# An attention block beside an MLP on one core: the MLP's second product by Strassen's algorithm, value products that leave PSUM batch by batch, mish in one bank, weights laid out by tiles

## The chip, the cores and the metric

The kernel runs on one core of one Trainium2 chip. The metric is the device time of one execution in microseconds; lower is better. Its engines are TensorE (PE; PEld is its weight load), VectorE (DVE), ScalarE (ACT), GpSimd (POOL) and SyncE (SP), which here only issues transfers (DMAs). Each engine works through its own instructions in order, and waits on semaphores for the others.

## The reference

```
xn = layernorm(x)                                  # x: 2048 x 1024
q, k, v = split(xn @ wqkv)                         # 32 heads of 32
s = concat(softmax(q k^T / sqrt(32)) v) @ wo
h = xn @ w1 + b1                                   # w1: 1024 x 3584
g = silu((h * tanh(softplus(h))) @ w2)             # mish; w2: 3584 x 1024
out = x + s * g
```

All of it is float32. The kernel splits each operand of a large product into a high and a low part in a shorter format (float32r) and adds three products (high x high, high x low, low x high): the constant THREE in the code. So a product of two 128 x 128 by 128 x 512 tiles is three matmuls.

## The kernel before

**Stages.** First the layer norm, the transposition of xn and the value projection (v, L324); meanwhile GpSimd splits the first 20 of 28 column tiles of w1 and stores the parts in DRAM (w1_early, w1s). Then the projections of q and k (qk, L623), 16 tiles f of four groups c of 24 matmuls; meanwhile GpSimd splits the other eight w1 tiles and all of w2 (presplit), and the parts go to DRAM (w2s). Then the main stage, in which attention and the MLP run interleaved. At last the output projection (op, L1113) with the gate, 768 matmuls.

**The main stage** is ordered by a planner written in the kernel (class Plan). Each engine has a list of operations with an assumed duration, what they need, which places of which ring they take and give (buffers and PSUM banks), and a due time; the planner plays this through and emits the instructions in the order that results. That order is then fixed for each engine. TensorE draws from five streams: s (scores by query, for the maxima, L694), t (scores by key, L781), h (first MLP product, L929), y (second MLP product, L1017), and at the end op.

**Attention.** For each head and each of 16 key tiles, t is made in four banks, ScalarE takes the exponential into a tile p of 128 x 2048 (L264), GpSimd adds p to the head's sum z (L810, 15 additions a head), and TensorE multiplies p with v (pv, L828) in three batches of 6, 5 and 5 key tiles (GROUPS), all into bank 7, which is kept for this. A p tile is free when both its addition and its batch are done. When the last addition of a head is done, TensorE multiplies z with ones (zp, L854) for the softmax denominator; there is one z tile, so the next head's first addition (z<-p,p) waits for that product. VectorE finds the maxima of s (mx, L700).

**MLP.** For each of four chunks of 512 rows and each of 28 column tiles of w1, h is made in 24 matmuls in one bank; mish is a chain of five ScalarE and seven VectorE operations (L948 to L984) which takes a second bank, q; its result is the pair of parts act. Two act tiles together are multiplied with two row tiles of w2: eight banks of six matmuls each, added to yacc by VectorE (L1037). w1 is read back in tiles of 1 MB with two places, w2 in tiles of 512 KB with five.

**Places.** w1_tile gives the split tiles of w1 and the qk weights (qkw) one of two places each. In the qk stage a group's result is copied by ScalarE (qst), its low part is taken by VectorE, and a DMA of ScalarE's queue stores it; the next tile's weights are split by ScalarE and VectorE in qk_split, which is written behind the first group of the tile before.

## Time and profile before

| | us |
|---|---|
| median of the runs (lowest, highest) | 3427.83 (3426.24, 3431.74) |
| the profiled execution | 3429.67 |
| its span, from the first to the last instruction | 3427.8 |
| TensorE busy | 3395.9 |
| GpSimd busy | 2461.5 |
| VectorE busy | 2320.4 |
| ScalarE busy | 1943.1 |
| first qk matmul (end of the v stage) | 214.64 |
| first output matmul of the last stage | 3248.98 |

All numbers of the prediction come from this one profiled execution. Its rows have these forms. A group of instructions: line, engine, operation, written tile <- read tiles, shape, count | busy us, mean ns of one | idle us of the engine just before them, and what ended most of it. A row of the timeline: start, length, engine, line, operation, tiles, count, and in brackets the idle time before it with the releaser. A row of a window: length; busy us and (count) of TensorE, its weight loads, VectorE, ScalarE, GpSimd; granted clock of TensorE; busy share of the 16 DMA engines; GB/s.

### The profile page before, as it was taken

Reading aid. Unit: us, or ns where it says so; the run is one execution under the profiler, and the core shown is the slowest. Engines: PE = TensorE matmul, PEld = TensorE weight load, DVE = VectorE, ACT = ScalarE, POOL = GpSimd, SP = SyncE. Lnnn points to the kernel's source line nnn. Section 1 sums busy time; section 2 is a strip of 40 time slices with the busy share of each in tenths; the row PEclk is TensorE's granted clock in tenths of the full one; section 3 lists DMA queues with packets and bytes.
Section 4 is the critical chain, followed back from the end, with each engine's and each line's share of the span. In section 5 each row is a group of like instructions: output and inputs, shape, how many; then the busy total and the mean of one; then the engine's idle time right before and its main releaser. Section 6 shows DMA issues by size and latency. Waiting matters only on the chain.

```text
span 3427.8 us, 47242 instructions
## 1 busy us (share of the span) xinstructions
PE 3395.9 (99%) x17827; PEld 2541.0 (74%) x17827; DVE 2320.4 (68%) x3750; ACT 1943.1 (57%) x3112; POOL 2461.5 (72%) x753
## 2 busy tenths in 40 slices
PE   8999999999999999999999999999999999999999
PEld 8998888676777777776777667777777777676787
DVE  6012236877878887887877777878788787874533
ACT  6111112666666667666666676666666666667621
POOL 0644342898888888888888788888888888888800
PEclk9999999999999999999999999999999999999999
DMA  8988897433433354343433543333435443433482
GB/s 290 299 297 299 295 316 236 124 107 91 124 111 111 99 164 147 109 120 103 124 111 111 159 137 111 111 110 113 127 104 167 131 129 109 116 113 129 151 289 85
DMA packets 294183, 529.71 MB, mean 155 GB/s; under 512 B 88810, under 2 KB 147178, under 8 KB 270186
## 3 DMA queue, kind: packets, MB, share of 16 engines
q1 hardware_dynamic: 274100, 484.74, 46.1%
q10 hardware_dynamic: 19856, 41.95, 3.3%
q8 instruction: 141, 2.31, 0.3%
q14 instruction: 86, 0.70, 0.1%
HBM read 386.89 MB, written 138.67 MB: 153 GB/s over the span
## 4 chain that ended last, share of the span: by engine, by line
PE 96%; DVE 1%; DMA 1%; ACT 1%; issue 0%; SPq 0%; POOL 0%; POOLq 0%
PE h L929 17%; PE y L1017 17%; PE t L781 13%; PE s L694 13%; PE pv L828 13%; PE qk L623 10%; PE op L1113 5%; PE v L324 5%; PE zp L854 1%; DVE mx L700 1%; PE s L550 0%; DMA qstack<-qs 0%; PE pt L379 0%; SPq L271 0%; DMA xr<-xs 0%
## 5 line engine op out<-in xcount | busy, mean ns | idle before, releaser
L810 POOL TENSOR_TENSOR z<-z,p 128x2048 f32<-128x2048 f32 x448 | 2065.4, 4610 | 197.4 <-ACT p L264 170.3
L264 ACT ACTIVATE p<-t,zero 128x512 f32<-128x512 f32 x2048 | 1377.6, 688 | 696.5 <-PE t L781 687.5
L700 DVE TENSOR_REDUCE mx<-s 128x1 f32<-128x512 f32 x1984 | 1318.6, 686 | 445.8 <-PE s L694 444.0
L1017 PE MATMUL y<-w,act 128*128 128x512 f32 x2688 | 928.3, 391 | 1.2 <-DVE yacc L1037 0.5
L781 PE MATMUL t<-qstack,kstack 128*128 128x512 f32 x2048 | 791.0, 392 | 3.3 <-DMA qstack<-mt 1.9
L694 PE MATMUL s<-kstack,qstack 128*128 128x512 f32 x1984 | 773.2, 395 | 9.8 <-issue 4.8
L929 PE MATMUL h<-xr,w 128*128 128x512 f32 x2016 | 698.5, 391 | 1.5 <-DMA xr<-xs 1.3
L1017 PEld LDWEIGHTS y<-w,act 128*128 128x128 f32 x2688 | 503.7, 188 | 115.0 <-issue 5.0
L694 PEld LDWEIGHTS s<-kstack,qstack 128*128 128x128 f32 x1984 | 368.0, 188 | 136.4 <-issue 43.3
L828 PE MATMUL pv<-p,v 128*32 128x512 f32 x4096 | 459.4, 595 | 0.0
L781 PEld LDWEIGHTS t<-qstack,kstack 128*128 128x128 f32 x2048 | 384.7, 188 | 97.1 <-issue 9.9
L929 PEld LDWEIGHTS h<-xr,w 128*128 128x128 f32 x2016 | 378.8, 188 | 84.1 <-issue 4.3
L623 PE MATMUL qk<-xc,qkw 128*128 128x512 f32 x1536 | 350.9, 390 | 0.0
L810 POOL TENSOR_TENSOR z<-p,p 128x2048 f32<-128x2048 f32 x32 | 147.9, 4621 | 261.8 <-ACT p L264 154.2
L828 PEld LDWEIGHTS pv<-p,v 128*32 128x32 f32 x4096 | 123.5, 110 | 282.2 <-issue 281.9
L623 PEld LDWEIGHTS qk<-xc,qkw 128*128 128x128 f32 x1536 | 288.3, 188 | 59.7
L1037 DVE TENSOR_TENSOR yacc<-yacc,y 128x512 f32<-128x512 f32 x416 | 283.1, 681 | 50.2 <-PE y L1017 49.0
L929 PE MATMUL h<-xc,w 128*128 128x512 f32 x672 | 233.1, 392 | 0.0
L275 DVE TENSOR_TENSOR qst<-qk,qst 128x512 fp32r<-128x512 f32 x64 | 44.2, 691 | 245.3 <-ACT qst L267 245.3
L267 ACT ACTIVATE qst<-qk 128x512 fp32r<-128x512 f32 x64 | 38.3, 598 | 300.1 <-PE qk L623 253.9
L324 PE MATMUL v<-vw,xc 128*128 128x256 f32 x1536 | 191.1, 286 | 2.5 <-POOL vw L275 1.5
L324 PEld LDWEIGHTS v<-vw,xc 128*128 128x128 f32 x1536 | 186.9, 193 | 4.1 <-POOL vw L275 1.9
(91 smaller groups left out, 2279.1 us busy)
## 6 DMA issues: line engine op xcount, KB each, us to landing
w<-w1s SPq DMA_DIRECT2D x112, 1024.0 KB
w<-w2s SPq DMA_DIRECT2D x224, 512.0 KB
w2s<-pw SPq DMA_DIRECT2D x56, 512.0 KB
qstack<-qs SPq DMA_DIRECT2D x96, 256.0 KB
kstack<-ks SPq DMA_DIRECT2D x96, 256.0 KB
w1s<-w1p SPq DMA_DIRECT2D x20, 1024.0 KB
praw<-in_B_w_dram SPq DMA_DIRECT2D x72, 256.0 KB
x<-in_A_x_dram SPq DMA_DIRECT2D x32, 512.0 KB
```

Source lines behind the costliest of these rows:

```text
L264: nc.scalar.activation(out_, in_, fn, bias=zero if bias is None else bias, scale=scale)
L324: nc.tensor.matmul(ps[:, :256], xc[t // 4][:, a, k, (t % 4) * P:(t % 4 + 1) * P], w[:, b, k], start=n == 0, stop=n == 3 * KT - 1)
L623: nc.tensor.matmul(ps, w[:, a, k], xc[c][:, b, k], start=n == 0, stop=n == 3 * KT - 1)
L694: nc.tensor.matmul(sp_, qst[h % 3][:, qt * P:(qt + 1) * P], kst[h % 3][:, kc * 512:(kc + 1) * 512], start=True, stop=True)
L700: nc.vector.reduce_max(tiles["mx"][:, qt, kc:kc + 1], tiles[qt, kc], axis=AX.X)
L781: nc.tensor.matmul(tp, kst[h % 3][:, kt * P:(kt + 1) * P], qst[h % 3][:, c * 512:(c + 1) * 512], start=True, stop=True)
L810: nc.gpsimd.tensor_tensor(zs[h], pts[T - 1] if kt == 1 else zs[h], pts[T], ALU.add)
L828: nc.tensor.matmul(pv[h][c * DH:(c + 1) * DH, :], vt[h][:, k, :], pts[T - kt + k][:, c * 512:(c + 1) * 512], start=k == 0, stop=k == NT - 1)
L929: nc.tensor.matmul(t["h"], w1t[n][:, a, k], xts_[c][:, b, k], start=i == 0, stop=i == 3 * KT - 1)
L1017: nc.tensor.matmul(t["y"], acts[n][:, p, s * P:(s + 1) * P], w2t[m_][:, q], start=j == 0 and i == 0, stop=j == YB - 1 and i == 2)
L1037: nc.vector.tensor_tensor(ya, ya, t["y"], ALU.add)
L1113: nc.tensor.matmul(ps[t, dh], ohl[t // 4, k][:, a, s * P:(s + 1) * P], wt[k][:, b, r], start=k == 0 and i == 0, stop=k == KT - 1 and i == 2)
```

## The change

**Strassen.** Two h tiles (a pair) and two halves of 256 rows make a 2 x 2 block matrix, and the two row tiles and two column halves of w2 another. Instead of eight block products the kernel makes seven (in Winograd's form of the algorithm). The sums of w2's blocks are made once, in the qk stage, and stored as seven parts a pair (w2_parts: four GpSimd subtractions, seven ScalarE copies, seven GpSimd low parts). The sums of the activations are made in the chain behind mish (g_copy, s1 to s4), in part by GpSimd (s2, and the low part of z). Each product is three matmuls for each of two row tiles, accumulated over all 14 pairs of a chunk in yacc, which has seven parts; at a chunk's end GpSimd adds them up in seven operations (y_sums).

**Value products.** Four batches of four key tiles, each into a bank of the common ring, which ScalarE (first batch) or VectorE (the others) at once adds to a tile in SBUF. So no bank is kept for it.

**mish** writes its square over h once that has been used (the tile n is new), and takes one bank instead of two.

**Weights** are brought into tile order on the host, so that a load reads long rows. 23 instead of 20 w1 tiles are split in the v stage. The split tiles and the qk weights take turns on two places (w_tile). w1 is read back in halves with three places, w2 with three places; p has six places instead of seven, and the planner's numbers are set anew.

```diff
-GROUPS, YB = (6, 5, 5), 2
+GROUPS = (4, 4, 4, 4)
...
-PS, ACTS, W2S, Y0, Y1 = 7, 3, 5, 1.2, 0.17
+PS, ACTS, W1S, W2S, Y0, Y1 = 6, 4, 3, 3, 1.2, 0.14
+YSEQ = (("x", 0), ("x", 1), ("y", 0), ("y", 1), ("z", 0), ("z", 1), ("w", 0))
-S_B, T_B, D_B = 2, 2, 5
+S_B, T_B, D_B = 3, 2, 5
...
-    def w1_tile(name):
-        return w1p.tile([P, 2, KT, P], F32R, tag="w1", name=name, bufs=2)
+    def w_tile(name):
+        w_made.append(name)
+        where, tag = ((w1p, "z0"), (big, "w"))[len(w_made) % 2]
+        return where.tile([P, 2, 2, KT // 2, P], F32R, tag=tag, name=name)
...
+    def w2_part(u, j, v):
+        w = pw_tile(f"pw2_{u}_{j}")
+        copy(w[:, 0], v)
+        low(nc.gpsimd, w[:, 1], v, w[:, 0])
+        later.at(1, lambda: move(w2s[u][:, j], w))
...
             qk_group(f, c if f < 2 * KT - 1 else (c + 1) % NC)
-            presplit()
-            if f % 2 and f < 14 and c in (0, 2):
+            if f < U:
+                w2_parts(f, c)
+                if c == 3 and f + 2 < U:
+                    later.at(1, lambda u=f + 2: w2_load(u))
+            if c == 3 and f < 2 * (FT - W1_V):
                 presplit()
             if c == 0 and f + 1 < 2 * KT:
                 qk_split(f + 1)
...
-                zs[h] = att.tile([P, S], F32, tag=f"z{at['z']}", name=f"z{h}")
+                zs[h] = w1p.tile([P, S], F32, tag="z0", name=f"z{h}")
...
+        def gather(at):
+            if kt == size - 1:
+                pv[h] = att.tile([P, 512], F32, tag=f"on{at['on']}", name=f"o{h}")
+                copy(pv[h], t["b"])
+            else:
+                nc.vector.tensor_tensor(pv[h], pv[h], t["b"], ALU.add)
...
+        def s3(at):
+            nc.vector.tensor_tensor(t["h"][:, R], t["h"][:, L], gs[n // 2][:, R], ALU.subtract)
+        def s1(at):
+            nc.vector.tensor_tensor(gs[n // 2][:, R], t["h"][:, R], gs[n // 2][:, R], ALU.add)
+        def s2(at):
+            nc.gpsimd.tensor_tensor(gs[n // 2][:, L], gs[n // 2][:, R], gs[n // 2][:, L], ALU.subtract)
+        def s4(at):
+            nc.vector.tensor_tensor(t["h"][:, L], t["h"][:, L], gs[n // 2][:, L], ALU.subtract)
...
+            nc.tensor.matmul(t["y"], acts[B, kind][:, p, half * 256 + s * P:half * 256 + (s + 1) * P],
+                             w2t[m_][:, q], start=i == 0, stop=i == 2)
...
+        def add_(i, j):
+            need = [last.get(x) or done[x, s] for x in (i, j) for s in range(2)]
+            o = op("POOL", 2.4, need=need, key=-1,
+                   emit=lambda at: nc.gpsimd.tensor_tensor(yacc[:, i], yacc[:, i], yacc[:, j], ALU.add))
```

**Where instructions move.** The first place is GpSimd at the end of the v stage. Before, in its order (w1p18 and w1p19 are split tiles of w1, w1e their raw values, qstack0 an attention tile that is cleared for later):

```order
L451 CAST w1p18_2444<-w1e18_2378 128x512
L275 TENSOR_TENSOR w1p18_2444<-w1e18_2378,w1p18_2444 128x512 [waits Pool_49]
L451 CAST w1p19_2513<-w1e19_2442 128x512 [waits DMAHW4_49,DMAHW2_49,Pool_49]
L275 TENSOR_TENSOR w1p19_2513<-w1e19_2442,w1p19_2513 128x512 [waits Pool_49]
L451 CAST w1p19_2513<-w1e19_2442 128x512
L275 TENSOR_TENSOR w1p19_2513<-w1e19_2442,w1p19_2513 128x512 [waits Pool_49]
L508 MEMSET qstack0_2719 32x2048 [waits PE_49,Pool_49]
```

And now, at the same place:

```order
L457 CAST w1p19_2501<-w1e19_2428 128x512
L282 TENSOR_TENSOR w1p19_2501<-w1e19_2428,w1p19_2501 128x512 [waits Pool_49]
L457 CAST w1p20_2565<-w1e20_2499 128x512 [waits DMAHW0_49,DMAHW7_49,DVE_49,PE_49]
L282 TENSOR_TENSOR w1p20_2565<-w1e20_2499,w1p20_2565 128x512 [waits Pool_49]
...
L457 CAST w1p21_2629<-w1e21_2563 128x512 [waits DMAHW3_49,DMAHW1_49]
...
L457 CAST w1p22_2691<-w1e22_2627 128x512 [waits DMAHW7_49,DMAHW5_49]
...
L514 MEMSET qstack0_2729 32x2048 [waits Pool_49]
```

Tiles 20 to 22 are new here. Tile 20 waits for TensorE (PE): its place, z0, is that of qk weight 0 (qkw0), which was asked for between w1 tiles 18 and 19, and the matmul waited for is the last one that reads qkw0, in the last group of the first qk tile.

The second place is ScalarE at the start of the qk stage. Before (vst3_15 is the last copy of the v stage, qst0_0 the first group's result, qkw1 the second qk tile's weights):

```order
L267 ACTIVATE vst3_15_2687<-v3_15_2688 128x256 [waits DMAHW7_49,PE_49,Activation_49]
L267 ACTIVATE qst0_0_2761<-qk0_0_2736 128x512 [waits DMAHW2_49,PE_49]
L267 ACTIVATE qkw1_2767<-qkraw1_2483 128x512 [waits DMAHW4_49,DMAHW5_49,DMAHW0_49,Pool_49]
L267 ACTIVATE qkw1_2767<-qkraw1_2483 128x512
L271 DMA qs0_62<-qst0_0_2761 128x2x512 [waits DMAHW1_49,DVE_49]
L267 ACTIVATE qst0_1_2800<-qk0_1_2775 128x512 [waits PE_49]
```

And now:

```order
L274 ACTIVATE vst3_15_2696<-v3_15_2697 128x256 [waits DMAHW0_49,PE_49,Activation_49]
L274 ACTIVATE qst0_0_2773<-qk0_0_2748 128x512 [waits DMAHW2_49,DMAHW7_49,PE_49,Pool_49]
L274 ACTIVATE pw2_0_0_2777<-raw2_0_2742 128x512 [waits DMAHW6_49]
L274 ACTIVATE pw2_0_2_2780<-raw2_0_2742 128x512 [waits DMAHW2_49]
L274 ACTIVATE qkw1_2783<-qkraw1_2469 128x512 [waits DMAHW5_49,DMAHW4_49,DMAHW1_49]
L274 ACTIVATE qkw1_2783<-qkraw1_2469 128x512
L278 DMA qs0_62<-qst0_0_2773 128x2x512 [waits DMAHW0_49,DVE_49]
```

The first result's copy now waits for GpSimd as well (for the end of w1 tile 22, on whose raw values its buffer lies), and two copies of w2's first pair (pw2) stand ahead of qkw1. Their load, raw2_0, is issued by SP behind the stores of w1 tiles 20, 21 and 22 and of the cleared tile.

The third place is GpSimd at a change of head in the main stage. Before (z4 and z5 are the sums of heads 4 and 5, p the exponentials, hl a small piece of a later head's maxima):

```order
L810 TENSOR_TENSOR z4_8653<-z4_8653,p79_9283 128x2048 [waits Activation_49,Pool_49]
L810 TENSOR_TENSOR z5_9449<-p80_9342,p81_9382 128x2048 [waits PE_49,Activation_49,Pool_49]
L810 TENSOR_TENSOR z5_9449<-z5_9449,p82_9445 128x2048 [waits Activation_49,Pool_49]
...
L275 TENSOR_TENSOR hl0_2727<-nm6_0_9722,hl0_2727 128x16 [waits Activation_49]
L810 TENSOR_TENSOR z5_9449<-z5_9449,p87_9712 128x2048 [waits Activation_49,Pool_49]
```

And now, between heads 9 and 10 (g34 is an operation s2, az17 a low part of z's activations):

```order
L848 TENSOR_TENSOR z9_13481<-z9_13481,p159_14049 128x2048 [waits Pool_49]
L848 TENSOR_TENSOR z10_14282<-p160_14095,p161_14142 128x2048 [waits PE_49,Activation_49,Pool_49]
L848 TENSOR_TENSOR z10_14282<-z10_14282,p162_14276 128x2048 [waits Activation_49,Pool_49]
L1060 TENSOR_TENSOR g34_14177<-g34_14177 128x256 [waits DVE_49]
L848 TENSOR_TENSOR z10_14282<-z10_14282,p163_14326 128x2048 [waits Activation_49,Pool_49]
L282 TENSOR_TENSOR az17_14364<-g34_14177,az17_14364 128x512 [waits Activation_49]
L848 TENSOR_TENSOR z10_14282<-z10_14282,p164_14375 128x2048 [waits Activation_49,Pool_49]
```

The pair's two operations now stand among the additions, and the first addition of a head waits for TensorE's z product as before.

More of the change, by code (lines that the diff above doesn't have):

```diff
@@ L165, in do @@
         op.places = places
+        pass
         op.emit(places)
@@ L518, in body @@
         nc.vector.memset(t.bitcast(F32), 0.0)
-    nc.vector.memset(early.tile([P, 48], F32, name="pad2"), 0.0)
     vt = {}
@@ L629, in qk_group @@
         later.at(1, lambda: move(dst, st, nc.scalar))
+    w2_load(0)
+    w2_load(1)
+    nc.vector.memset(early.tile([P, 48], F32, name="pad2"), 0.0)
     for f in range(2 * KT):
@@ new lines, in hi, with emit, lo @@
+        def hi(kind, r, src):
+            def emit(at):
+                ring = "aw" if kind == "w" else "act"
+                if (n // 2, kind) not in acts:
+                    w = 256 if kind == "w" else 512
+                    acts[n // 2, kind] = mlp.tile([P, 2, w], F32R, tag=f"{ring}{at[ring]}", name=f"a{kind}{n // 2}")
+                copy(acts[n // 2, kind][:, 0, r], src()[:, r])
+            return emit
+        def lo(kind, r, src, eng=None):
+            def emit(at):
+                a = acts[n // 2, kind]
+                low(eng or nc.vector, a[:, 1, r], src()[:, r], a[:, 0, r])
+            return emit
@@ L993, in mish @@
         p4 = op("ACT", 0.73, need=[p3], emit=a4)
         o4 = op("DVE", 0.69, need=[p4], emit=d4)
[L995 to L1000 removed]
+        o5 = op("DVE", 0.69, need=[o4], emit=d5, give=["r"])
@@ L1002, in y_stream @@
+    made_by, gs = {}, {}
+    yacc = mlp.tile([P, 7, 2, 512], F32, name="yacc")
     def y_stream():
@@ L1034, in y_add @@
                         if b == 0:
-                            copy(ya, t["y"])
+                            copy(ya, t["y"], scale=-1.0)
                         else:
-                            nc.vector.tensor_tensor(ya, ya, t["y"], ALU.add)
-                    done.append(op("DVE" if b else "ACT", 0.69 if b else 0.6, emit=y_add, urgent=U_Y, give=[("d", t["own"]), ("b", t["own"])],
-                                   need=[m] + ([ys_ops[c - 1]] if b == 0 and c else [])))
-            if b == FT // YB - 1:
-                def store(at, c=c):
-                    nc.sync.dma_start(ys[c], yacc)
-                ys_ops[c] = op("SP", 0.1, need=done, emit=store, bytes_=P * 4096 * 4)
```

344 lines of the change are left out of this document (214 added, 130 removed).

## The prediction

> **What bounds the kernel now.** I read the page first, then the busy time of the main stage (from the first to the last softmax denominator, the z products), then the costliest groups.
>
> ```profile
> span 3427.8 us, 47242 instructions
> ...
> PE 3395.9 (99%) x17827; PEld 2541.0 (74%) x17827; DVE 2320.4 (68%) x3750; ACT 1943.1 (57%) x3112; POOL 2461.5 (72%) x753
> ```
> ```profile
> 672.00:3244.00 2572.00, 2561.45 (x13335) 1828.31 (x13331) 2004.17 (x3195) 1712.19 (x2708) 2156.98 (x498) 1.00 0.41 121
> ```
>
> In the window's row the numbers behind the length are the busy times of TensorE, its weight loads, VectorE, ScalarE and GpSimd. TensorE idles 11 of 2572 us, so nothing shortens this stage but less TensorE work. VectorE stands at 78%, GpSimd at 84%: room, but not much. The groups that the change touches, or that it leans on:
>
> ```profile
> L1017 PE MATMUL y<-w,act 128*128 128x512 f32 x2688 | 928.3, 391 | 1.2 <-DVE yacc L1037 0.5
> L810 POOL TENSOR_TENSOR z<-z,p 128x2048 f32<-128x2048 f32 x448 | 2065.4, 4610 | 197.4 <-ACT p L264 170.3
> L810 POOL TENSOR_TENSOR z<-p,p 128x2048 f32<-128x2048 f32 x32 | 147.9, 4621 | 261.8 <-ACT p L264 154.2 <-PE zp L854 101.5 <-ACT mt L267 6.1
> ```
>
> A matmul's 391 ns is not its price, since matmuls overlap. The price is the distance between starts, read where one kind runs alone (the chain of waits):
>
> ```profile
> 482.13 5.44 PE qk L623 x24
> ```
>
> 5.44 / 24 = 0.2267 us.
>
> **The change, part by part.** *TensorE.* The second product falls from 2688 to 56 pairs x 7 products x 2 row tiles x 3 = 2352 matmuls: 336 x 0.2267 = 76.2 us less. The value product (pv) goes from three batches a head to four, and a batch has a cost of its own:
>
> ```profile
> 1437.90 0.39 PE L929 MATMUL h<-xr,w 128*128 128x512 f32 x1
> 1438.22 5.36 PE L828 MATMUL pv<-p,v 128*32 128x512 f32 x48
> 1443.51 0.74 PE L694 MATMUL s<-kstack,qstack 128*128 128x512 f32 x2
> 1444.09 0.40 PE L781 MATMUL t<-qstack,kstack 128*128 128x512 f32 x1
> ...
> 1464.31 0.61 PE L929 MATMUL h<-xr,w 128*128 128x512 f32 x2
> 1464.86 4.50 PE L828 MATMUL pv<-p,v 128*32 128x512 f32 x40
> 1469.28 0.73 PE L694 MATMUL s<-kstack,qstack 128*128 128x512 f32 x2
> 1469.85 0.63 PE L781 MATMUL t<-qstack,kstack 128*128 128x512 f32 x2
> ...
> 1501.26 1.04 PE L854 MATMUL zp<-z,ones 128*32 128x512 f32 x8
> 1502.23 0.33 PE L527 MATMUL mtp<-ident_r,hl 128*128 128x128 f32 x1
> ```
>
> Beyond the neighbours' own starts the batch of six key tiles takes 5.51 us (5.38 to the next start, 0.13 late after it) and the batch of five 4.64: 0.87 a tile and 0.3 a batch. 32 more batches cost 10 us. TensorE's work falls by **66 us**.
>
> *VectorE* gets 312 more y additions (728 instead of 416; the first of each chunk of rows are ScalarE copies), 96 additions of value products, and four half-wide operations for each of 56 pairs. Its operations follow each other at 0.60 us:
>
> ```profile
> 1005.55 0.68 DVE L1037 TENSOR_TENSOR yacc<-yacc,y 128x512 f32<-128x512 f32 x1
> 1006.14 0.69 DVE L868 SCALAR_TENSOR_TENSOR zp<-zp,rz 128x512 f32<-128x512 f32 x1
> 1006.74 1.28 DVE L700 TENSOR_REDUCE mx<-s 128x1 f32<-128x512 f32 x2
> ```
>
> 408 x 0.60 = 245 us, and 224 half-wide ones at 0.35 (an estimate; a full one is 0.60) 78: 2004 + 323 = 2327 of some 2520 us, 92%. That still fits beside TensorE, and shorter pv batches starve it for less at a time; mish holding one bank instead of two returns banks. No term, but it is one reason for the slack below. *ScalarE* (1712 of 2572 us) gets one full and three half copies more a pair and 24 y copies; at 0.60 us for each of the 248 (a full copy's time in a row below) that is 149 us, 74% of the stage: covered by what it waits for today. The last chunk's sums (17 us) and stores lie beside the output stage's 768 x 0.2267 = 174 us, which needs them in its last quarter.
>
> *GpSimd* is the engine that I fear. Its additions of a head start when the z product has read the single z tile, and that product waits for the head's last addition. So from z product to z product the time is the longer of two sums: TensorE's work in that stretch, and 15 additions plus the wait at the change of head.
>
> ```profile
> 1339.70 4.63 POOL L810 TENSOR_TENSOR z<-p,p 128x2048 f32<-128x2048 f32 x1 [5.75 <-PE zp L854]
> 1344.40 18.64 POOL L810 TENSOR_TENSOR z<-z,p 128x2048 f32<-128x2048 f32 x4
> ```
> ```profile
> L275 POOL TENSOR_TENSOR pw<-praw,pw 128x512 fp32r<-128x512 f32 x72 | 94.1, 1307 | 5.8
> L275 POOL TENSOR_TENSOR vw<-vraw,vw 128x1024 fp32r<-128x1024 f32 x7 | 16.6, 2389 | 69.2 <-ACT vw L267 69.2
> ```
>
> Additions follow each other at (18.64 - 4.61) / 3 = 4.67 us. The wait of 5.75 holds a batch of five; with four it is 4.88. New on GpSimd: for each pair one 256-wide and one 512-wide operation (about 0.7, half of the pw row and a little, and 1.3), and seven 1024-wide sums (2.4) for each chunk of rows. I counted both sums, head by head, in the two orders. Before, TensorE's sum is 2550 us (measured: 2572) and GpSimd's 2354, with TensorE the longer in all 31 stretches. After, 2484 against 2469, and GpSimd is the longer in 12. The clearest inner one: between the z products of heads 9 and 10 TensorE has 252 single matmuls (57.1), 16 key tiles (13.9), 4 batches (1.2) and a z product (1.0) = 73.2 us, since it worked ahead while GpSimd did the sums of a chunk in head 8; GpSimd has 15 x 4.67 + 2.0 + 4.88 = 76.9. The differences add up to **28 us** (10 of them in the last head, 68.9 against 78.9). At the other end, with 4.61 an addition, 4.5 for the wait and the cheapest prices, they are 15; with the mean wait of today's heads, 261.8 / 32 = 8.2, they are 92. I take 28: 5.75 is the row in which nothing but the z product was waited for.
>
> *The border between the v and the qk stage.* 23 instead of 20 weight tiles of the first product are now split early, and these share two places with the qk weights in strict turns. By the order, w1 tile 20 takes the place of qk weight 0, so GpSimd waits until TensorE has read that for the last time, at the end of the first of 16 qk tiles. TensorE's next operand, qk weight 1, stands on ScalarE behind a copy that waits for GpSimd's tile 22 and behind two copies of a w2 tile, whose load is queued on SP behind the stores of tiles 20 to 22. Nothing else is queued for TensorE. Today the same work is done while it runs:
>
> ```profile
> 216.19 0.61 POOL L451 CAST w1p<-w1e 128x512 fp32r<-128x512 f32 x1 [6.60 <-DMA w1s<-w1p]
> 216.88 1.30 POOL L275 TENSOR_TENSOR w1p<-w1e,w1p 128x512 fp32r<-128x512 f32 x1
> 218.12 0.62 POOL L451 CAST w1p<-w1e 128x512 fp32r<-128x512 f32 x1
> 218.81 1.30 POOL L275 TENSOR_TENSOR w1p<-w1e,w1p 128x512 fp32r<-128x512 f32 x1
> 220.17 1.80 POOL L508 MEMSET qstack<- 32x2048 f32 x1
> ```
> ```profile
> 220.15 0.60 ACT L267 ACTIVATE qst<-qk 128x512 fp32r<-128x512 f32 x1 [1.30 <-PE qk L623]
> 224.11 1.15 ACT L267 ACTIVATE qkw<-qkraw 128x512 fp32r<-128x512 f32 x2 [3.36 <-DMA w1s<-w1p]
> ```
>
> A tile is 3.9 us of GpSimd, a megabyte lands 4.0 us after its last write (220.1 to 224.1). From TensorE's last read: three tiles 11.7 (the third also waits for the first one's store, 3.9 + 4.0 = 7.9), the memset 1.8, the load of w2 4.0 (to 8, behind the third store), two copies 1.2, half of qk weight 1 on ScalarE and VectorE 1.3: 20 to 24 us of bare wait. The restart costs a little too:
>
> ```profile
> 577.31 0.33 PE L527 MATMUL mtp<-ident_r,hl 128*128 128x128 f32 x2
> 578.77 0.50 PE L694 MATMUL s<-kstack,qstack 128*128 128x512 f32 x1 [1.12 <-ACT mt L267]
> ...
> 581.36 0.63 PE L781 MATMUL t<-qstack,kstack 128*128 128x512 f32 x1
> 581.78 0.63 PE L929 MATMUL h<-xc,w 128*128 128x512 f32 x1
> ```
> ```profile
> 582.00:584.00 2.00, 2.00 (x6) 1.55 (x6) 0.27 (x1) 1.37 (x2) 0.00 (x0) 0.54 1.27 200
> ```
>
> After some 3 us with hardly a matmul the starts lie 0.42 apart and the granted clock is 0.54, for about eight matmuls: 1.6 us. The Trainium skill (TensorE: Matmul & The Clock Gate, Part 1) says that the clock halves after an idle window of about 3.4 us and returns after as much work. By that rule the border pays it once and the heads' waits, nearly all shorter, never; the row shows a drop after two waits of about 1.1 us close together, so by the row the heads of 3 us and more could pay 1.6 each, some 5 us in all, and the sum would be that much higher. With the restart I take **22 us** (20 to 28).
>
> *The qk stage's transfers.* In a qk tile's 96 x 0.2267 = 21.8 us the queues now move four 512 KB stores of q or k, seven 512 KB stores of w2 products, a 1024 KB and a 512 KB load, and in the first ten tiles 768 KB of w1: 7936 KB, 8.13 MB, 373 GB/s. The trace shows
>
> ```profile
> 456.00:478.00 22.00, 22.00 (x99) 18.23 (x98) 4.28 (x6) 3.43 (x6) 11.40 (x12) 1.00 0.95 334
> ```
>
> 334 GB/s at 95% (the last two columns), 352 if full: 23.1 us a tile, 1.3 more over nine tiles, 12 us. The weights now come in long rows instead of 512-byte ones, which may win that back: **2 us**, range 0 to 14. The same layout and the bias could gain up to 6 us of the idle at the very start.
>
> *Slack.* The w2 tiles (three places instead of five, 392 loads instead of 224), VectorE at 92%, the halved w1 tiles: each was covered, and is so still by smaller margins. **2 us**, range 0 to 18.
>
> Sum: -66 + 28 + 22 + 2 + 2 = -12, so a span of 3416. That execution took 3429.67 us with its launch, 1.8 more than its span and 1.8 more than the median of the runs; these cancel, and the forecast for the median is **3416**. Differences under 0.2%, about 7 us, are what a measurement of this kernel can't tell from none.
>
> **The rivals.** *A, GpSimd never holds TensorE up:* its new operations fall into the wait for the z product. For it: 11 of the 31 stretches have one there by the order. Against: the additions alone and that wait are 74.9 us of 80. -66 + 22 + 2 + 2 = -40: 3388; with all that the start could gain 3376. *B, GpSimd becomes the bound (slower):* at the change of head it waits 8.2 us, as today's heads do on average, because the exponentials come late from six places for p instead of seven. Against: today those waits are for a TensorE that is itself the bound. -66 + 92 + 26 = +52: 3480; it decides from a wait of about 5.7 us, where the heads' sum passes 40. *C, the transfers (slower):* qk tiles at the DMA's pace and late w2 tiles, all upper ends: -66 + 28 + 28 + 14 + 18 = +22: 3450. For it: 95% now. Against: TensorE never waits in that row.
>
> **How the numbers follow.** Forecast 0.46, A 0.22, B 0.17, C 0.15. The forecast's own bounds are 3397 to 3440 (15 and 20 at the low end). The range 3376 to 3460 leaves out B and a little of C. Faster: A and 0.64 of the forecast, 0.51; same: 0.30 of the forecast, 0.14; slower: the rest, 0.35.
>
> **What would show it.** Right: y with 2352 matmuls; one idle stretch of TensorE of 20 us or more near 236 us, ended by ScalarE's or VectorE's qkw; GpSimd near 92% with some 5 us before each z<-p,p; TensorE's idle in the main stage 40 us instead of 11. Wrong: no such stretch at the border, waits at z<-p,p near 8 us (B), or qkw and w2 waits all along the qk and main stages (C).

## The result and the profile after

The changed kernel takes 3483.86 us (median of 4 runs, 3481.06 to 3487.33) against 3427.03 of the kernel before beside it: ratio 1.0164, interval 1.0146 to 1.0181. It is slower, and outside the forecast's range. Its profiled execution spans 3480.5 us, 52.7 more than before. The page of the changed kernel begins:

```profile
span 3480.5 us, 48746 instructions
...
PE 3369.9 (97%) x17491; PEld 2470.6 (71%) x17491; DVE 2616.7 (75%) x4382; ACT 2072.4 (60%) x3458; POOL 2731.0 (78%) x935
```

TensorE works less and idles more: 110.6 us of the span against 31.9. To see where, two rows mark the stages: those of the qk matmuls and of the products with ones (least, median and greatest duration in ns, then the first and last start in us). Before:

```profile
L623 PE MATMUL qk<-xc,qkw x1536: 388/390/447, 214.5 to 576.2; 128*128 128x512 f32 x192
...
L854 PE MATMUL zp<-z,ones x256: 592/592/617, 672.2 to 3244.3; 128*32 128x512 f32 x128
```

After:

```profile
L653 PE MATMUL qk<-xc,qkw x1536: 387/389/796, 214.5 to 650.2; 128*128 128x512 f32 x192
...
L903 PE MATMUL zp<-z,ones x256: 592/592/593, 743.1 to 3297.1; 128*32 128x512 f32 x128
```

The qk stage starts at the same time and ends 74.0 us later. From its end to the first product with ones 3.1 us come back, and the main stage is 18.1 us shorter (2554.0 for 2572.1). The rest, the output, takes 183.4 us instead of 183.5. 74.0 - 3.1 - 18.1 - 0.1 = 52.7: **the whole loss lies in the qk stage**.

A window of that stage before, from 280 to 560 us, and the same after:

```profile
280.00:560.00 280.00, 280.00 (x1237) 231.96 (x1236) 87.08 (x130) 42.94 (x78) 115.87 (x120) 1.00 0.88 301
```
```profile
280.00:560.00 280.00, 247.72 (x1042) 197.83 (x1040) 59.20 (x69) 82.50 (x148) 178.97 (x145) 0.96 0.90 327
```

TensorE, which had no gap there, now does 1042 matmuls instead of 1237, at a granted clock of 0.96. The longest waits of TensorE and of ScalarE in the changed kernel from 214 to 580 us are (total, count, longest; s, L554, are the scores of head 0, which run among the last qk tiles)

```profile
PE qk L653 <- ACT qkw L274: 44.4, 9, 25.0
PE s L554 <- DVE qst L282: 4.8, 2, 3.4
PE s L554 <- DVE mx L558: 4.7, 1, 4.7
PE qk L653 <- DVE qkw L282: 3.4, 6, 1.0
```
```profile
ACT pw L274 <- DMA w2s<-pw: 114.2, 25, 15.6
ACT pw L274 <- POOL tmp L632: 68.2, 28, 2.9
ACT qst L274 <- POOL w1p L282: 36.1, 1, 36.1
```

One wait of 25.0 is the forecast's border stall. The others are not at the border: 23 us are waits for the qk weight, which comes late again and again, and ScalarE, which makes it, waits for stores of w2's products. The scores of head 0 wait 9.5 us for VectorE's work on the groups' results and on their maxima.

The border, in the timelines of TensorE, GpSimd and ScalarE (changed kernel):

```profile
214.52 21.95 PE L653 MATMUL qk<-xc,qkw 128*128 128x512 f32 x96
261.47 0.80 PE L653 MATMUL qk<-xc,qkw 128*128 128x512 f32 x1 [25.01 <-ACT qkw L274]
...
236.53 0.61 POOL L457 CAST w1p<-w1e 128x512 fp32r<-128x512 f32 x1 [28.29 <-PE qk L653]
...
251.26 0.60 ACT L274 ACTIVATE qst<-qk 128x512 fp32r<-128x512 f32 x1 [36.11 <-POOL w1p L282]
259.75 0.63 ACT L274 ACTIVATE pw<-raw 128x512 fp32r<-128x512 f32 x1 [7.90 <-DMA raw<-in_B_w_dram]
...
260.81 1.13 ACT L274 ACTIVATE qkw<-qkraw 128x512 fp32r<-128x512 f32 x2
```

Read from left to right in time: TensorE finishes the first qk tile at 236.5, GpSimd starts w1 tile 20 at once, ScalarE is let go by GpSimd at 251.3, then by the load of w2 at 259.8, and qk weight 1 follows at 260.8. That is the forecast's chain, step by step. Behind it TensorE runs at half its clock for 5 us:

```profile
261.50:266.50 5.00, 5.00 (x12) 3.72 (x13) 3.12 (x3) 1.55 (x3) 4.26 (x4) 0.50 0.44 144
```

Further on, around the change to another tile, ScalarE and TensorE:

```profile
403.82 1.14 ACT L274 ACTIVATE qkw<-qkraw 128x512 fp32r<-128x512 f32 x2
405.74 0.60 ACT L274 ACTIVATE qst<-qk 128x512 fp32r<-128x512 f32 x1 [0.79 <-DMA ks<-qst]
414.55 0.63 ACT L274 ACTIVATE pw<-tmp 128x512 fp32r<-128x512 f32 x1 [8.21 <-DMA w2s<-pw]
...
404.48 15.80 PE L653 MATMUL qk<-xc,qkw 128*128 128x512 f32 x67 [2.62 <-ACT qkw L274]
428.52 0.73 PE L653 MATMUL qk<-xc,qkw 128*128 128x512 f32 x2 [1.67 <-ACT qkw L274]
```

A split product (pw) has three places. Each is free when its store has landed, and while ScalarE waits for one (8.2 us here), the results of qk groups and the next qk weight stand behind it in its order. From 404.48 to 428.52 a tile takes 24.0 us where TensorE needs 21.8.

In the main stage the changed kernel's window reads

```profile
743.10:3297.10 2554.00, 2521.24 (x12998) 1754.17 (x12994) 2270.32 (x3800) 1780.26 (x2941) 2313.81 (x630) 1.00 0.53 157
```

VectorE stands at 89%, GpSimd at 91%. GpSimd's two rows of additions, over the whole page:

```profile
L848 POOL TENSOR_TENSOR z<-z,p 128x2048 f32<-128x2048 f32 x448 | 2067.1, 4614 | 76.0 <-ACT p L271 51.5
...
L848 POOL TENSOR_TENSOR z<-p,p 128x2048 f32<-128x2048 f32 x32 | 147.8, 4620 | 189.6 <-PE zp L903 111.8
```

Its waits for exponentials in the first row fell to 51.5 us (170.3 before), and the wait for the product with ones is 111.8 us over 32 heads. To weigh TensorE's waits of well under 1 us, which the window's busy time hides in part, I added up in the trace by how much the distance between the starts of two neighbouring single matmuls (s, t, h, y) exceeds 0.2267 us, without the few distances in which a record is missing. That gives 25 us before and 74 after. What is left of the stage, 2547 and 2480, is TensorE's own work: **67 us less**. So of those 67 us 49 went into small waits.

### The profile page after: what moved, and what is told of

Its sections match the earlier page's. It is cut to its first block, busy times and chain, and to the rows that moved or that the text cites. A ratio compares the mean times of both kernels' runs of the same rounds, so it can differ in the third digit from the quotient of the medians.

```text
span 3480.5 us, 48746 instructions
## 1 busy us (share of the span) xinstructions
PE 3369.9 (97%) x17491; PEld 2470.6 (71%) x17491; DVE 2616.7 (75%) x4382; ACT 2072.4 (60%) x3458; POOL 2731.0 (78%) x935
## 4 chain that ended last, share of the span: by engine, by line
PE 79%; DVE 7%; DMA 6%; POOL 4%; issue 2%; ACT 2%; SPq 0%; ACTq 0%; POOLq 0%; DVEq 0%
PE h L978 16%; PE y L1119 13%; PE pv L867 12%; PE s L732 12%; PE t L819 12%; PE v L329 5%; PE op L1246 4%; PE qk L653 3%; DMA w2s<-pw 3%; DVE mx L738 2%; POOL pw L282 1%; POOL z L848 1%; DVE yacc L1142 1%; DMA kstack<-ks 1%; DVE qkw L282 1%
## 5 line engine op out<-in xcount | busy, mean ns | idle before, releaser
L848 POOL TENSOR_TENSOR z<-z,p 128x2048 f32<-128x2048 f32 x448 | 2067.1, 4614 | 76.0 <-ACT p L271 51.5
L738 DVE TENSOR_REDUCE mx<-s 128x1 f32<-128x512 f32 x1984 | 1286.4, 685 | 69.0 <-PE s L732 66.5
L732 PE MATMUL s<-kstack,qstack 128*128 128x512 f32 x1984 | 755.9, 397 | 17.8 <-DMA kstack<-ks 5.6
L978 PE MATMUL h<-xr,w 128*128 128x512 f32 x2016 | 678.5, 391 | 1.6 <-DMA xr<-xs 0.6
L1142 DVE TENSOR_TENSOR yacc<-yacc,y 128x512 f32<-128x512 f32 x728 | 493.9, 682 | 38.0 <-PE y L1119 34.8
L653 PE MATMUL qk<-xc,qkw 128*128 128x512 f32 x1536 | 365.8, 398 | 48.1 <-ACT qkw L274 44.4
L848 POOL TENSOR_TENSOR z<-p,p 128x2048 f32<-128x2048 f32 x32 | 147.8, 4620 | 189.6 <-PE zp L903 111.8
L1119 PE MATMUL y<-w,az 128*128 128x512 f32 x672 | 232.2, 395 | 5.4 <-POOL az L282 2.4
L1119 PE MATMUL y<-w,ay 128*128 128x512 f32 x672 | 226.9, 391 | 3.4 <-ACT ay L274 1.3
L1119 PE MATMUL y<-w,ax 128*128 128x512 f32 x672 | 225.0, 392 | 2.8 <-DMA w<-w2s 1.1
L978 PE MATMUL h<-xc,w 128*128 128x512 f32 x672 | 224.8, 390 | 0.0
```

The source lines that it names most:

```text
L653: nc.tensor.matmul(ps, w[:, k // 4, a, k % 4], xc[c][:, b, k], start=n == 0, stop=n == 3 * KT - 1)
L732: nc.tensor.matmul(sp_, qst[h % 3][:, qt * P:(qt + 1) * P], kst[h % 3][:, kc * 512:(kc + 1) * 512], start=True, stop=True)
L738: nc.vector.reduce_max(tiles["mx"][:, qt, kc:kc + 1], tiles[qt, kc], axis=AX.X)
L848: nc.gpsimd.tensor_tensor(zs[h], pts[T - 1] if kt == 1 else zs[h], pts[T], ALU.add)
L978: nc.tensor.matmul(t["h"], w1t[m_][:, a, k % 4], xts_[c][:, b, k], start=i == 0, stop=i == 3 * KT - 1)
L1119: nc.tensor.matmul(t["y"], acts[B, kind][:, p, half * 256 + s * P:half * 256 + (s + 1) * P], w2t[m_][:, q], start=i == 0, stop=i == 2)
```

## The experiments

Times are set beside the changed kernel's 3483.86; ratios are against the kernel before, in runs on the same chip.

**e1, the border alone.**

```diff
-            if i == 3 and t == 7:
+            if i == 3 and t == NT - 2:
                 qk_split(0)
```

> Edit: the changed kernel, but the first qk weight is split at v tile 14 of the last group instead of tile 7, so that the two shared weight places hold w1 tiles 20 to 22 before it and not after it. In the changed kernel's trace TensorE waits 25.0 us for a qk weight near 236 us. Theory (the border stall is a wait of its own, caused by the turns of the two places): the 25 us wait goes, at most 3 us come in front of the first qk matmul, and the time falls by 20 to 27 us, to about 3460. Rival (the qk stage is set by its transfers, so that what is gained at the border is given back later): the last qk matmul still starts within 8 us of 650, and the time falls by less than 8 us.

3459.32 us, 24.5 less (ratio 1.0093, 1.0077 to 1.0108), within the theory's 20 to 27. But the qk stage now starts 8.1 us late, behind the store of a w1 tile, where at most 3 were expected. It ends 26.7 earlier:

```profile
L653 PE MATMUL qk<-xc,qkw x1536: 387/389/796, 222.6 to 623.5; 128*128 128x512 f32 x192
```

The stall is a wait of its own, and nothing of it is given back later.

**e2, six places for the split products.**

```diff
-        return sp.tile([P, 2, 512], F32R, tag="pw", name=name, bufs=3)
+        pw_made.append(name)
+        if len(pw_made) % 2:
+            return sp.tile([P, 2, 512], F32R, tag="pw", name=name, bufs=3)
+        return w1p.tile([P, 2, 512], F32R, tag="w1", name=name, bufs=W1S)
```

> Edit: the changed kernel with six places instead of three for the split second weights of the qk stage (every second one uses a place of the first product's weight ring, which is empty then). In the changed kernel TensorE waits 20 us for qk weights behind the border (44.4 in all, less the 25.0), and ScalarE's copies, ahead of the qk weight's, wait 114 us for stores of earlier products. Theory (coupling: three places and the latency of a store hold ScalarE, and with it the qk weight): the waits of ScalarE for those stores fall below 40 us, TensorE's waits for qk weights behind the border below 5, and the time falls by 15 to 45 us, with the transfers moving over 350 GB/s from 280 to 560 us. Rival (bytes: the stage moves what the DMA engines can): the stores only queue longer, the qk stage ends within 8 us of 650, and the time falls by under 8 us.

3442.62 us, 41.2 less (ratio 1.0041, 1.0029 to 1.0054), with the border stall still in it. The window from 280 to 560 us, and the waits of TensorE and ScalarE in the stage:

```profile
280.00:560.00 280.00, 274.77 (x1202) 226.44 (x1201) 82.27 (x105) 91.51 (x163) 206.76 (x161) 0.99 0.98 367
```
```profile
PE qk L658 <- ACT qkw L274: 24.4, 1, 24.4
PE s L554 <- DVE mx L558: 3.5, 1, 3.5
PE s L554 <- DVE qst L282: 1.8, 1, 1.8
...
ACT pw L274 <- DMA w2s<-pw: 9.0, 3, 6.2
```

Before the qk matmuls only the border's wait is left, the scores of head 0 still wait 5.3 us, ScalarE's waits for the stores fell from 114 to 9, and the same transfers now move 367 GB/s at 98%. From 280 to 400 us, where no scores run, they move 388 GB/s and TensorE never idles:

```profile
280.00:400.00 120.00, 120.00 (x532) 99.37 (x531) 28.87 (x33) 40.18 (x71) 96.13 (x76) 1.00 1.01 388
```

The stage ends at 611.1 instead of 650.2, 39 us sooner. So the DMA engines could move this stage's bytes faster than the changed kernel let them; the three places held them back. The coupling theory holds.

**e3, fewer bytes while w2 is split.**

```diff
-            if c == 3 and f < 2 * (FT - W1_V):
+            if f >= 14 or f == 13 and c % 2:
                 presplit()
```

> Edit: the changed kernel with the ten late split jobs of the first product's weights (a load of 256 KB and a store of 512 KB each) moved from qk tiles 0 to 9 to tiles 13 to 15, where few second weights are split. Over tiles 0 to 9 a tile moves 7.3 MB instead of 8.1, that is 338 GB/s at TensorE's 21.8 us a tile instead of 373. Bytes theory: tiles 0 to 9 run at TensorE's pace but for the border, and the time falls by 15 to 25 us, to about 3463. Coupling theory (places and latency): two of the nine operations that take a place are gone from each tile, so a part of the waits goes: 5 to 15 us. Rival that neither holds (the waits come from the order of ScalarE's copies alone): under 5 us.

3453.24 us, 30.6 less (ratio 1.0071, 1.0059 to 1.0084), more than either theory gave.

```profile
280.00:560.00 280.00, 271.66 (x1186) 223.73 (x1186) 86.61 (x104) 89.31 (x164) 184.30 (x139) 0.98 0.92 336
```

336 GB/s is the 338 that the smaller load asks for at TensorE's pace. ScalarE still waits 97.6 us for stores here, but no longer long enough to make a weight late; the scores of head 0 still wait 8.3 us. So 373 GB/s through three places is too much, and either side can be eased.

**e4, a second place for the sums z,** gave no time: its 8 KB a partition lie in another pool, and of the 52 KB that the pool of the attention's tiles takes only 44.5 were then left. It was to take GpSimd's wait for the product with ones (111.8 us) away and with it 20 to 45 us of the main stage. So no run shows what this wait costs.

**e5, all three, with the border mended without the late start.** The edits of e2 and e3, and

```diff
-                early_w1[f - 1][1] = w = w_tile(f"w1p{f - 1}")
-                split_w(w, raw, True)
+                if f < 20:
+                    early_w1[f - 1][1] = w = w_tile(f"w1p{f - 1}")
+                    split_w(w, raw, True)
+                else:
+                    early_w1[f - 1][1] = w = [w1p.tile([P, 2, KT // 2, P], F32R, tag="w1", name=f"w1p{f - 1}_{i}",
+                                                       bufs=W1S) for i in range(2)]
...
```

> Edit: the changed kernel with the six places of e2, the late split jobs moved as in e3, and at the border w1 tiles 19 to 22 split into the three empty half places of the first product's ring, so that the two shared places go to qk weights 0 and 1 at once (no late start of the first qk matmul, which came 8 us later in e1). The main stage is as in the changed kernel. Coupling and bytes theory (qk stage lost 74 us: 25 at the border, some 40 to places and bytes): the last qk matmul starts between 577 and 592 (before: 577), the time falls by 58 to 74 us from the changed kernel, to 3410 to 3426, and so the change's own loss against before was the qk stage's. Rival (the gains overlap, since each of them frees the same DMA time): the time falls by under 50 us, and the stage moves more than 355 GB/s from 280 to 560.

3419.34 us, 64.5 less than the changed kernel, and a little less than the kernel before (ratio 0.9976, 0.9967 to 0.9985). The gains of e2 and e3 overlap, as they must: each removes the same waits.

```profile
L671 PE MATMUL qk<-xc,qkw x1536: 389/389/447, 214.5 to 576.2; 128*128 128x512 f32 x192
...
280.00:560.00 280.00, 280.00 (x1237) 231.85 (x1236) 94.31 (x129) 88.28 (x158) 180.56 (x139) 1.00 0.93 334
...
L921 PE MATMUL zp<-z,ones x256: 592/592/593, 679.2 to 3234.8; 128*32 128x512 f32 x128
```

The qk stage is back at 214.5 to 576.2, to the tenth of a microsecond that of before, with w2's seven products split in it. The main stage is as long as the changed kernel's (2555.6). Of the 74 us won 10 go again between the two stages: from the last qk matmul to the first product with ones it takes 103.0 us instead of 92.9, with 7.0 us of waits for a load of the attention (qstack, in place of 0.6) and a granted clock of 0.93 instead of 1.00. What is left to explain is why the main stage gains only some 17 us.

**e6, GpSimd lighter in the same order** (changed kernel; the eighth addition of each head is left out, and one is added to the denominators).

```diff
+            if kt != 8:
                 nc.gpsimd.tensor_tensor(zs[h], pts[T - 1] if kt == 1 else zs[h], pts[T], ALU.add)
```

> Edit: the changed kernel in its own order, with the eighth of the 15 additions of each head left out on GpSimd (the denominators lack key tile 8, and one is added to them before the logarithm so that none is zero). GpSimd has 4.7 us less in each head, and nothing else moves. Theory (GpSimd sets the pace in a part of the heads of the main stage): the stage from the first to the last product with ones, 2554 us in the changed kernel, falls by 30 to 65 us, towards the 2484 of TensorE's own work, and TensorE's waits fall. Rival (VectorE, at 89%, or the places in PSUM hold TensorE): it falls by under 10 us, and GpSimd idles 145 us more.

3483.51 us, ratio 1.0161 (1.0147 to 1.0175). The total is the same and the main stage 5.4 us shorter, although GpSimd has 143 us less to do; that is the rival's range:

```profile
742.70:3291.30 2548.60, 2520.00 (x12998) 1754.47 (x12994) 2267.16 (x3799) 1778.64 (x2941) 2170.45 (x599) 1.00 0.53 157
```

In this order GpSimd doesn't hold TensorE. The theory falls in the form that it had.

**e7, GpSimd's two operations a pair on VectorE.** `lo("z", ...)` and `s2` with nc.vector instead of nc.gpsimd.

> Edit: the changed kernel with the two operations that each pair of tiles puts on GpSimd (the half-wide subtraction and the low part of the third operand) on VectorE instead, planned anew. GpSimd loses 56 x 1.9 = 106 us, or 3.4 us a head, and VectorE gets 56 x 0.95 = 53 us and goes from 89% to 91% of the main stage. GpSimd theory: the main stage falls by 20 to 45 us. Rival (VectorE is as near to its limit as GpSimd, and the stage only changes its bound): within 10 us either way. Second rival (VectorE holds TensorE already): it grows by over 10 us.

3676.27 us (ratio 1.0727, 1.0712 to 1.0741): 192 us more, far beyond the "over 10" of the second rival, and for a reason that no theory had. VectorE's rows of the moved operations in e7, and rows of the same size with one operand in PSUM in the changed kernel:

```profile
L1060 DVE TENSOR_TENSOR g<-g 128x256 f32<-128x256 f32 x56 | 130.4, 2329 | 0.3
L282 DVE TENSOR_TENSOR az<-g,az 128x512 fp32r<-128x512 f32 x56 | 120.7, 2155 | 0.4 <-ACT az L274 0.4
```
```profile
L282 DVE TENSOR_TENSOR ax<-h,ax 128x512 fp32r<-128x512 f32 x56 | 38.4, 686 | 2.8 <-ACT ax L274 2.5
L1054 DVE TENSOR_TENSOR h<-h,g 128x256 f32<-128x256 f32 x56 | 24.0, 428 | 5.0 <-ACT g L274 4.4
```

With both operands in SBUF an operation takes 2.2 us on average, some 1.5 to 1.9 more than its like, beside additions of 4.6 us on GpSimd. The average hides two cases: those that began while GpSimd did nothing (9 of the 56 with 256 columns, 23 of the 56 with 512) took 0.41 to 0.43 and 0.67 to 0.68 us, as their like, and the others, but for three, ended just after GpSimd's instruction (the last section shows one). (2.33 - 0.43 + 2.16 - 0.69) x 56 = 189 us, about as much as the loss; what the new order adds of its own was not measured. So e7 measured a price of that place, and says nothing on GpSimd's pace.

**e8, the sums at a chunk's end on VectorE.** `y_sums` with nc.vector. The planner puts the seven sums of a chunk in another order there, so that the result is another; the work is the same.

> Edit: the changed kernel with the seven 1024-wide sums of each chunk of rows on VectorE instead of GpSimd. In the changed kernel the three stretches between products with ones that hold these sums take 105.5, 102.2 and 100.3 us on GpSimd, and the others 80.2 on average. GpSimd theory: those three stretches fall to about 90 each (7 x 2.4 = 17 us less on GpSimd), and the main stage falls by 20 to 45 us; the stretches behind them, in which TensorE had worked ahead, lose the lead. Rival (TensorE works ahead meanwhile, and what is gained there is given back in the next heads): the main stage falls by under 10 us.

3500.35 us (ratio 1.021, 1.0196 to 1.0223), 16 more, where the theory had a fall and the rival a small one. Here, too, 10 of the 28 sums waited for an instruction of GpSimd (up to 5.5 us; the other 18 took 1.2), though the order is another as well:

```profile
L1155 DVE TENSOR_TENSOR yacc<-yacc 128x1024 f32<-128x1024 f32 x28 | 63.8, 2294 | 0.3
```

**e9, VectorE lighter in the same order,** on e5's kernel; three of seven y additions are left out.

```diff
-                        else:
+                        elif j not in (1, 3, 6):
                             nc.vector.tensor_tensor(ya, ya, t["y"], ALU.subtract)
```

> Edit: the kernel of e5 in its own order, with VectorE's additions for three of the seven products of each pair left out (but for the first pair of a chunk): 324 additions of 0.60 us, so VectorE has 194 us less in the main stage, about as much as the change put there; the output lacks what they add. Theory (VectorE, at 89% of the stage and read in order by everything that holds a place in PSUM, is what gives TensorE its many waits under 1 us): the main stage, 2556 us in e5, falls by 35 to 75, towards TensorE's own 2484. Rival (the order of the work on TensorE and the places in PSUM themselves, or ScalarE): it falls by under 10 us, and VectorE idles 190 us more.

3414.67 us (ratio 0.9961, 0.9946 to 0.9976). The main stage is 2547.8, 7.8 less than e5's, with VectorE at 2105 us instead of 2267 (312 additions fewer by the trace, not 324). That is the rival's range and not the theory's 35 to 75:

```profile
680.50:3228.30 2547.80, 2518.64 (x12998) 1755.11 (x12994) 2105.14 (x3490) 1778.69 (x2941) 2312.94 (x630) 1.00 0.53 157
```

**e10, both lighter in the same order.** e9 and e6 together.

> Edit: e9 with e6's edit besides (the eighth addition of each head left out on GpSimd, one added to the denominators before the logarithm). If VectorE alone holds TensorE, the main stage stays within 8 us of e9's. If GpSimd stands close behind VectorE, as the one next to bind (it waits for TensorE's products with ones at most heads in e5), it falls by another 15 to 45 us.

3417.0 us (ratio 0.9963, 0.9949 to 0.9976), main stage 2550.9, as e9. The engines' loads, in this order, are not what TensorE waits for.

**e11, four places for scores.** `S_B, T_B, D_B = 4, 2, 5` on e5's kernel, planned anew.

> Edit: the kernel of e5 with scores allowed four of the eight places in PSUM instead of three, planned anew. Places theory (TensorE waits 0.3 to 1 us before scores since all three of their places wait for VectorE's maxima): the main stage falls by 10 to 40 us. VectorE theory (the maxima come late, whatever the number of places): within 10 us either way. Rival (a fourth place for scores is taken from the second product): it grows by 10 us or more.

3446.33 us (ratio 1.0052, 1.0039 to 1.0065). The main stage grows by 21 us, to 2576.5, as the rival said, and TensorE's small waits to 87. These are only 9 of the 21 us, and which of the other products misses the place was not followed.

**e12, no gathering of value products,** on e5's kernel: VectorE's additions in `gather` are left out.

> Edit: the kernel of e5 in its own order, without VectorE's additions of the second to fourth value product of each head (the output lacks three of the four). That is only 96 x 0.60 = 58 us of VectorE, where e9 took 194 away, but each of them waits in VectorE's order for a batch of value products (109 us of waiting in e5's main stage, the largest of VectorE's), with maxima and other work that frees places in PSUM behind it. Coupling theory (TensorE's waits under 1 us come of engines that wait for each other in a fixed order, and the additions of value products are the chief place): the main stage falls by 25 to 50 us, more than the 8 of e9. Rival (the order of the plan itself, with its 2 places for transposed scores and 3 for scores, holds TensorE at many small places): it falls by under 10 us, like e9.

3421.26 us (ratio 0.9979, 0.997 to 0.9989), main stage 2555.3, as long as e5's. The largest of VectorE's waits is not the place either.

**e13, e14, e15: new orders.** In e13 the plan counts e9's left-out additions at 0.09 us, in e14 it counts e6's left-out one at nothing (both on e5's kernel), and e15 does both.

> Edit: e9 planned anew: the plan counts the left-out additions at 0.09 us instead of 0.69, so that the order of all engines is made for a VectorE with 194 us less. Order theory (the order was written for a VectorE that is nearly full, and in that order less work gains nothing): the main stage falls by 30 us or more from e9's 2548, towards 2484. Rival (a new order meets the same places in PSUM, and TensorE's small waits stay): within 12 us of 2548.

3418.93 us (ratio 0.9971, 0.9962 to 0.9981), main stage 2551.5, which is in the rival's range. But the new order changed what TensorE waits for. Of the small waits those that VectorE ends fell from 16 us (e9) to 7, and those that a load ends rose from 12 to 34. The longest row of TensorE's waits in the main stage, in e9 and in e13 (kstack holds a later head's keys):

```profile
PE s L750 <- DMA kstack<-ks: 7.8, 6, 2.7
```
```profile
PE s L750 <- DMA kstack<-ks: 21.7, 16, 3.1
```

So e13 shows that this order gains nothing, and not what a lighter VectorE would gain if the loads came in time.

> Edit: the kernel of e5 with e6's edit (the eighth addition of each head left out on GpSimd, one added to the denominators), and planned anew with that addition counted at nothing. Theory (the order of all engines is written to GpSimd's pace, so that less work on it counts only in a new order): the main stage, 2556 us in e5, falls by 12 to 35 us. Rival (a new order meets the same few places in PSUM): it stays within 8 us of e6's 2549.

3408.22 us (ratio 0.9947, 0.9931 to 0.9964):

```profile
681.10:3212.00 2530.90, 2506.47 (x12993) 1751.95 (x12985) 2262.70 (x3793) 1777.18 (x2936) 2167.94 (x598) 1.00 0.53 158
```

The main stage is 2530.9, **25 us less** than e5's, and the small waits fall from 78 to 54. The same lighter GpSimd that gained nothing in the old order gains this in a new one. How much an order changes from one plan to the next by itself was not measured.

> Edit: e14 and e13 together: GpSimd lighter by 145 us and VectorE by 194, and the order planned for both. Theory (both engines near their limits make the order's waits, each alone being relieved in vain): the main stage falls below 2520, and TensorE's waits between single matmuls, 78 us in e5, below 50. Rival (places in PSUM: scores, transposed scores, first and second product share eight): within 15 us of e9's 2548, with more than 60 us of such waits.

3407.7 us (ratio 0.9942, 0.9927 to 0.9957), main stage 2538.6, small waits 61. The theory fails: the stage stays over 2520 and the waits over 50, and both numbers are those of the rival, within 15 us of 2548 with more than 60 us of waits. With less work than e14 the stage is 7.7 us longer, so an order can come out that much worse with less to do, and of e14's 25 us some may be the order's own.

## Why the prediction was wrong

**The step that failed is "the qk stage's transfers: 2 us, range 0 to 14".** It compared a demand of 373 GB/s with a capacity of 352 and took the difference as the price. What it left out is that the bytes go through three places, each held until its store has landed, and that the engine which waits for a place, ScalarE, also makes the next qk weight, later in the same order. The stage lost 74.0 us. 25.0 are the border's wait, and behind it the clock is 0.50 for another 5 us (about 2.6 us of loss); the other 46 are set down to this term. By the trace they are 23 us of waits for the qk weight, 9.5 of waits of head 0's scores, and some 14, the rest, of a lower clock behind such waits. Six places (e2) take 39 of the 46 away, 5.3 of the rest being waits of those scores; why these come late no run separates. Rate alone would not have cost it: e2 moves 388 GB/s from 280 to 400 us, over the supposed 352 and over the demand of 373, and TensorE does not wait there.

Of the other terms:

- *TensorE, -66:* right. The stage's work without small waits is 67 us less, and the y matmuls number 2352 (three groups of 672, one of 336).
- *The border, +22 (20 to 28):* right in mechanism, and in size within its range: 25.0 us of wait and 2.6 behind it, 24.5 us in e1.
- *GpSimd, +28 (15 to 92):* the size is near e14's 25 us, by chance as far as the runs show, and the mechanism stood a level too low. I had counted the two engines' sums head by head in the order, and expected GpSimd to stop TensorE when the kernel runs. It doesn't (e6). What e14 suggests is that the order itself had been written to its pace, and that the time is lost in that order. GpSimd's share was 91% (forecast 92), its wait for TensorE ahead of z<-p,p 3.5 us a head (111.8 / 32) rather than 5, and TensorE's idle time in the stage's window 33 us rather than 40.
- *Slack, +2 (0 to 18):* too small. Of the 49 us of small waits, some 24 are not explained by e14. By the semaphores in the trace VectorE ends 23 us of the 74 (2 before) and loads end 9 (1.5 before). Taking work from VectorE in the same order removes few of them (e9, e12), in a new order it trades them for waits for loads (e13), and a place more for scores makes it worse (e11). That leaves the eight places in PSUM, shared by more kinds of tile than before, and the loads of the main stage; no run has separated them, and this part stays open.

With the measured terms, -67 + 25 + 24 + 27.6 + 46.4, less 3.1 between the stages, the sum is +53. It closes by construction, since 24 and 46.4 are what was left of 49 and of 74.0.

The rivals: B gave 3480, next to the result, but by coincidence, since its mechanism did not happen: the waits at the change of head are 3.5 us, not 8.2, and the main stage became shorter. C had the right place, waits for qkw all along the stage, and this half of its sign was seen (waits for w2 in the main stage came to 2.9 us); but it priced them by bytes at 14 us. A, that GpSimd never holds TensorE, is true of the run and, as far as e14 shows, not of the order.

## What to carry to other kernels

Work that is moved into a stage is priced by the loop that it closes, not by bytes over rate alone: how many places there are, how long each is held (until the store has landed), and what else stands behind the waiting instruction on its engine. Here three places instead of six cost some 40 us at 90% of the DMA engines' time. And in an order that is fixed ahead, taking work off an engine shows only what that engine costs in this order; whether it sets the pace of the plan is seen only when the order is made again without it, and then one has to look at what the new order waits for (e13).

## What the runs showed of the hardware

**VectorE beside GpSimd.** In e7 an operation of VectorE with both operands in SBUF took 0.41 us (256 columns) or 0.68 (512) when GpSimd did nothing, and up to 4.8 when it was adding. The first row is one that began while GpSimd was idle, the second one that began 0.49 us after the addition in the third:

```profile
1264.87 0.41 DVE L1060 TENSOR_TENSOR g<-g 128x256 f32<-128x256 f32 x1
...
1310.59 4.38 DVE L1060 TENSOR_TENSOR g<-g 128x256 f32<-128x256 f32 x1
```
```profile
1310.10 4.59 POOL L848 TENSOR_TENSOR z<-z,p 128x2048 f32<-128x2048 f32 x1
```

The addition ends at 1314.69, the operation at 1314.97, 0.28 us later. All but two of the 47 that began while GpSimd worked end 0.28 to 0.30 us after its instruction, and of the 33 such with 512 columns all but one end 0.55 or 0.56 us after it. The wait lies inside the duration and shows as no idle time. The Trainium skill (SBUF — State Buffer, Who interferes with whom) says that a VectorE instruction with two inputs in SBUF contends with a GpSimd instruction that reads SBUF, and that the ports which the two share are an exclusive lock. The trace agrees, by these 0.28 and 0.55 us.

**The clock.** In the changed kernel's qk stage the granted clock fell after a wait far shorter than the border's. Two windows around the wait of 1.67 us at 428.52:

```profile
427.00:430.00 3.00, 1.29 (x4) 0.78 (x5) 1.96 (x3) 2.06 (x5) 3.00 (x3) 1.00 0.96 354
430.00:434.00 4.00, 4.00 (x12) 3.13 (x11) 1.69 (x2) 0.46 (x1) 1.36 (x3) 0.57 1.05 379
```

TensorE was busy 1.29 of 3 us, and then ran 12 matmuls in 4 us. The Trainium skill (TensorE: Matmul & The Clock Gate, Part 1) speaks of an idle window of about 3.4 us. Here the drop followed a stretch of 3 us that was 43% busy, with no gap longer than 1.67 us. So a wait at a tile's change can cost more than its length: from 400 to 580 us the granted clock was 0.92 on average, which comes to some 14 of the 46 us.
